# Opening by chunk: the first image loaded chunk by chunk, tiles 0 to 3 with stationary values, row sums in column groups and a listed order

## Chip, cores, metric

One core of one Trainium2 chip. The metric is device time in microseconds (us) of one execution, median of several. Ratios are the mean time of one kernel's runs over the mean of the other's runs of the same rounds, so they are not quite the ratio of the medians quoted beside them. Under 1 means faster than the kernel before.

## The reference

An attention over pooled keys is followed by a gated feed-forward block. Keys and values are the same matrix.

```
B, C, Hh, Ww = 4, 128, 384, 32;  r = 4;  d_ff = 1536
kv_pool = kv.reshape(B, H//r, r, W//r, r, C).mean(axis=(2, 4))     # 4x4 pixels -> one key
k = v = kv_pool.reshape(B, -1, C) @ w_sr                          # 768 keys an image
a = exp(q @ k^T / sqrt(C)) / row sum;   x = a @ v                 # 12288 queries an image
out = (max(x @ w_gate, 0) * (x @ w_val)) @ w_out
```

One image row of kv has 32 pixels of 512 bytes, 16 KB. A **chunk** is 128 keys, so 64 full image rows or the same number of pixels, 1 MB; an image has six. A **tile** is 512 queries, 256 KB; there are 96, numbered 0 to 95. To **turn** is to transpose, an **issue** is the instruction that starts a transfer, and a **packet** is a piece of a transfer as the trace records it.

## The kernel before

The change touches only the opening: the loads of the first image, the attention of tiles 0 to 3, and their order. Behind it runs a loop over tiles that both kernels share. Before, two chunks came together in four transfers (one for each of the four lines `dh` of the 4x4 blocks):

```python
def kv_load(b, pair, queues=(nc.sync,)):
    parts = work.tile([128, r, 2, r, C], FP32, tag="kv_in", bufs=3)
    rows = kv[b, pair * 2 * HC : (pair + 1) * 2 * HC].rearrange(
        "(hp dh) (wp h dw) c -> dh hp wp (h dw c)", dh=r, h=2, dw=r      # 32 x 4 runs of 4 KB
    )
    for dh in range(r):
        queues[dh % len(queues)].dma_start(parts[:, dh].rearrange("p h dw c -> p (h dw c)"), rows[dh])

def q_load_plain(i0, i1):                   # tiles 0-1 and 2-3: 128 runs of 4 KB, one after the other
    nc.sync.dma_start(q32, q[0, i0 * T : i1 * T, :].rearrange("(p i s) c -> p i s c", i=i1 - i0, s=NS))

def q_load_tile(i):                         # tiles 4 and 5 only
    nc.sync.dma_start(q32, q[0, i * T : (i + 1) * T, :].rearrange("(t j s) c -> j t (s c)", j=4, s=NS))
...
kv_load(0, 0, (nc.sync, nc.scalar))
nc.sync.dma_start(w_sr_f32, w_sr)
for i in range(0, GRP, 2):
    q_load_plain(i, i + 2)
for pair in range(1, NJC // 2):
    kv_load(0, pair)
for i in range(GRP, GRP + 2):
    q_load_tile(i)
```

The value step had the exponentials stationary, four matmuls of 128 x 129 for each chunk of keys, with the row sum as column 129; the tile was then normalised and turned:

```python
def values(k, jc, half):
    ...
    for i in range(2):
        s = 2 * half + i
        nc.tensor.matmul(x_ps[:, i, :], aTs[k][:, jc, s * 128 : (s + 1) * 128],
                         kv16[:, k // NST, jc, C : 2 * C + 1], ...)
...
fill(4)                                     # four idle matmuls
s1 = add_pixels(add_lines(0))               # VectorE adds the lines of two chunks at once
...                                         # turn, project, cast and turn queries, then
scores_of(0, 0)
scores_of(1, 0)
...
```

The softmax here doesn't subtract the row's maximum and nothing guards it: scores larger than these inputs give would overflow.

## Time and profile before

| | before |
|---|---|
| time | 1031.94 us (1031.92 to 1032.3) |
| TensorE busy in the profiled execution | 1022.0 of 1030.3 us |
| first score matmul starts (timeline) | 13.68 us |
| first output projection of tile 0 starts (timeline) | 37.86 us |

The last row marks the start of the shared loop. The chain of waits puts the same two starts at 13.73 and 38.02, because a step of the chain begins where the one before it ends; for comparisons below I use the timeline's figures throughout. The busy table, the stretches and the chain of this kernel are shown in the prediction. These are the two transfers of tiles 4 and 5, and the casts that wait for them (columns: durations min/median/max in ns, first and last start in us):

```profile
L109 SPq DMA_DIRECT2D q_tile<-in_q_dram x2: 583/624/664, 13.2 to 14.5; - x2
L119 POOL CAST q<-q_tile x2: 613/613/613, 24.8 to 29.4; 128x512 f16<-128x512 f32 x2
```

They were issued at 13.2 and 14.5, behind the keys, whose bytes were through at about 21 us. The casts could start only at 24.8 and 29.4, that is 4.6 us apart for 256 KB, or 57 GB/s. Nothing waited for them in this kernel, so nothing was lost. The change loads tiles 0 to 3 in the same way.

### The profile page before, as it was taken

The numbers are of one execution on the slowest core, as the hardware profiler recorded it, in microseconds if no ns is written. First come the engines' busy times: TensorE is split into PE (matmuls) and PEld (weight loads), VectorE is DVE, ScalarE is ACT, GpSimd is POOL, SyncE is SP. The second block draws the span as 40 slices with busy tenths as digits, with TensorE's granted clock in tenths as the row PEclk, the third lists the DMA queues.
The fourth block names the chain that finished last, engine by engine and source line by source line (L and its number), as shares of the span: only waits on it lengthen the run. The fifth ranks groups of instructions, "written<-read, shape, count | busy, mean of one in ns | idle before, by whom it ended". The sixth has DMA issues, their size and how long they took to land.

```text
span 1030.3 us, 20013 instructions
## 1 busy us (share of the span) xinstructions
PE 1022.0 (99%) x6560; PEld 543.7 (53%) x6560; DVE 913.0 (89%) x1676; ACT 909.3 (88%) x1745; POOL 280.5 (27%) x289
## 2 busy tenths in 40 slices
PE   7999999999999999999999999999999999999998
PEld 4555555555555555555555555555555555555555
DVE  4889898998989898998989898999888898989898
ACT  4989988888998888888888899888889988889887
POOL 1312146521211124642212121664121221111110
PEclk9999999999999999999999999999999999999999
DMA  8936396462543547726355266783653534513222
GB/s 317 120 60 81 91 191 143 77 93 42 85 65 52 78 121 161 169 52 91 52 67 85 35 85 139 144 171 57 86 65 55 73 53 67 87 33 64 34 42 53
DMA packets 328896, 93.60 MB, mean 91 GB/s; under 512 B 308568, under 2 KB 321752, under 8 KB 328792
## 3 DMA queue, kind: packets, MB, share of 16 engines
q1 hardware_dynamic: 313672, 78.24, 39.6%
q0 software_dynamic: 14688, 12.98, 11.0%
q8 instruction: 51, 0.84, 0.3%
q10 hardware_dynamic: 432, 1.11, 0.3%
q14 instruction: 53, 0.43, 0.1%
HBM read 53.94 MB, written 26.35 MB: 78 GB/s over the span
## 4 chain that ended last, share of the span: by engine, by line
PE 98%; DMA 1%; DVE 0%; ACT 0%; issue 0%; SPq 0%; ACTq 0%
PE bank_ps L298 24%; PE bank_ps L309 24%; PE bank_ps L333 23%; PE bank_ps L260 13%; PE bank_ps L249 12%; PE bank_ps L319 1%; DMA parts<-in_kv_dram 1%; PE bank_ps L182 0%; PE bank_ps L208 0%; PE bank_ps L200 0%; DVE kv_s L499 0%; DVE kv_s L460 0%; SPq L156 0%; PE bank_ps L136 0%; PE bank_ps L291 0%
## 5 line engine op out<-in xcount | busy, mean ns | idle before, releaser
L312 DVE SCALAR_TENSOR_TENSOR hT<-bank_ps,val 128x512 f16<-128x512 f32 x1152 | 758.0, 687 | 90.8 <-ACT val L302 70.3
L302 ACT CAST val<-bank_ps 128x512 f16<-128x512 f32 x1152 | 677.5, 589 | 102.2 <-PE bank_ps L298 100.2
L298 PE MATMUL bank_ps<-xT,wv 128*128 128x512 f16 x1152 | 436.6, 379 | 0.1
L309 PE MATMUL bank_ps<-xT,wg 128*128 128x512 f16 x1152 | 436.6, 379 | 0.0
L333 PE MATMUL bank_ps<-hT,wo 128*128 128x512 f16 x1116 | 423.0, 379 | 0.0
L250 ACT ACTIVATE aT<-bank_ps 128x512 f16<-128x512 f32 x576 | 345.4, 603 | 1.5 <-PE bank_ps L249 1.2
L343 POOL TENSOR_SCALAR o_sb<-o_t 128x512 f32<-128x512 f32 x93 | 138.3, 1487 | 694.0 <-DVE rinv L268 688.8
L260 PEld LDWEIGHTS <-aT 128*128 128x128 f16 x2304 | 177.0, 98 | 132.4
L260 PE MATMUL bank_ps<-kv,aT 128*128 128x129 f16 x2304 | 222.8, 220 | 0.0
L249 PE MATMUL bank_ps<-qT,kv 128*128 128x512 f16 x576 | 216.7, 379 | 0.2 <-DVE qT L139 0.2
L298 PEld LDWEIGHTS <-wv 128*128 128x128 f16 x1152 | 112.7, 98 | 132.2
L309 PEld LDWEIGHTS <-wg 128*128 128x128 f16 x1152 | 112.7, 98 | 67.3 <-DVE x L276 0.2
L333 PEld LDWEIGHTS <-wo 128*128 128x128 f16 x1116 | 109.2, 98 | 65.7
L249 PEld LDWEIGHTS <-kv 128*128 128x128 f16 x576 | 56.1, 98 | 67.8 <-issue 0.7
L276 DVE TENSOR_TENSOR x<-bank_ps,rinv 128x256 f16<-128x256 f32 x190 | 80.6, 425 | 6.6
L341 DVE STREAM_TRANSPOSE o_t<-bank_ps 128x512 f32<-128x512 f32 x93 | 65.7, 706 | 0.0
L86 POOL DMA_DIRECT2D q<-in_q_dram x84 | 46.0, 553 | 0.3 <-issue 0.3
L167 POOL TENSOR_TENSOR s<-parts 128x512 f32<-128x512 f32 x36 | 44.8, 1265 | 0.1
L268 DVE RECIPROCAL rinv<-bank_ps 128x2 f32<-128x2 f32 x192 | 28.2, 147 | 1.2 <-PE bank_ps L260 1.2
L169 POOL TENSOR_TENSOR s<-s 128x512 f32<-128x512 f32 x18 | 22.8, 1266 | 1.4
L171 POOL TENSOR_TENSOR c<-s 128x256 f32<-128x256 f32 x18 | 13.1, 725 | 1.4
L319 PEld LDWEIGHTS <-hT 128*128 128x128 f16 x144 | 10.2, 98 | 5.8
(54 smaller groups left out, 97.1 us busy)
## 6 DMA issues: line engine op xcount, KB each, us to landing
parts<-in_kv_dram SPq DMA_DIRECT2D x46, 512.0 KB, 6.5
out_dram<-o_sb SPq DMA_DIRECT2D x353, 64.0 KB, 2.2
q<-in_q_dram POOLq DMA_DIRECT2D x84, 128.0 KB, 4.8
xT<-x SPq DMA_TRANSPOSE x94, 2.5
out_dram<-o_sb SPq DMA_DIRECT2D x80, 16.0 KB, 1.5
placed<-blocks SPq DMA_DIRECT2D x9, 128.0 KB, 1.9
kvT<-placed SPq DMA_DIRECT2D x36, 32.0 KB, 1.9
parts<-in_kv_dram ACTq DMA_DIRECT2D x2, 512.0 KB, 7.4
```

Of the source, the lines that this page charges most:

```text
L86: nc.gpsimd.dma_start(q16[32 * j : 32 * (j + 1)].rearrange("t (i s) c -> t i s c", i=GRP), rows[j])
L249: nc.tensor.matmul(s_ps, kv16[:, k // NST, jc, 0:C], qT_of(k), start=True, stop=True)
L250: nc.scalar.activation(aTs[k][:, jc, :], s_ps, AF.Exp, scale=qk_scale)
L260: nc.tensor.matmul(x_ps[:, i, :], aTs[k][:, jc, s * 128 : (s + 1) * 128], kv16[:, k // NST, jc, C : 2 * C + 1], start=(jc == 0 and i == 0) ...
L276: nc.vector.tensor_tensor(x16s[k][:, 2 * half : 2 * half + 2, :], x_ps[:, :, 0:C], rinv.to_broadcast([128, 2, C]), op=ALU.mult,)
L298: nc.tensor.matmul(va_ps, wv16[:, fb * 128 : (fb + 1) * 128], xTs[k], start=True, stop=True)
L302: nc.scalar.copy(val, va_ps)
L309: nc.tensor.matmul(g_ps, wg16[:, fb * 128 : (fb + 1) * 128], xTs[k], start=True, stop=True)
L312: nc.vector.scalar_tensor_tensor(hTs[k][:, fb, :], g_ps, 0.0, vals.pop((k, fb)), op0=ALU.max, op1=ALU.mult)
L333: nc.tensor.matmul(o_banks[k], wo16[:, fb, :], hTs[k][:, fb, :], start=fb == 0, stop=fb == NFB - 1)
L341: nc.vector.transpose(o_t, o_banks.pop(k))
L343: nc.gpsimd.tensor_scalar(o_sb.rearrange("t j s c -> t s j c"), o_t.rearrange("t (s j c) -> t s j c", s=NS, j=4), 1.0 / X_SCALE**2, None, ...
```

## The change

Its intent is to start earlier and to idle less: chunks come one by one, so that the first score needs 1 MB of keys, not 2; tiles 0 to 3 use values as the stationary operand (512-column matmuls, output already turned); their row sums are made by 32-row matmuls of ones in four column groups; normalisation moves to the end as a scale by the inverse square of the sum; and all steps of the opening stand in one listed order. Cut to its core:

```diff
+    OPENING = """
+        a0 T0.3 cast1 qt1 b0 p0 a1 cast3 qt3 T0.p kvT0 qT1 pj0 qT3 key0 cast0 gate20 W0 W1 cast4
+        ...                                     # S = score, V = value, v/g = projections, U = row sums
+        g0.7 v0.5 g0.0 V1.4 v0.9 g0.2 V1.5 v0.8 g0.5 V2.4 v0.1 g0.9 S4.3 xT1 V2.5 g0.8 v0.6
+        g0.11 S4.1 g0.1 v0.10 V2.3 g0.4 S4.0 xT2 g0.6 g0.10
+    """.split()
...
+    def kv_load_lines(chunk, lines, queues=(nc.sync,)):
+        rows = kv[0, chunk * HC : (chunk + 1) * HC].rearrange(
+            "(hp dh) (wp dw) c -> dh hp wp (dw c)", dh=r, dw=r         # 16 x 8 runs of 2 KB
+        )
+        for dh in lines: ...dma_start(kv_in[0, pair][:, dh, h]..., rows[dh])
...
+    def lead_values(k, jc):
+        nc.tensor.matmul(x_banks[k], kv16[:, 0, jc, C : 2 * C], aTs[k][:, jc, :], ...)
+    def lead_sums(chunks):
+        for jc in chunks:
+            for k in range(LEAD):
+                nc.tensor.matmul(x_banks["sums"][32 * k : 32 * (k + 1), :], ones, aTs[k][:, jc, :],
+                                 ..., tile_position=(0, 32 * k))
...
-    kv_load(0, 0, (nc.sync, nc.scalar))
+    kv_load_lines(0, range(r), (nc.sync, nc.scalar))
     nc.sync.dma_start(w_sr_f32, w_sr)
-    for i in range(0, GRP, 2):
-        q_load_plain(i, i + 2)
-    for pair in range(1, NJC // 2):
-        kv_load(0, pair)
-    for i in range(GRP, GRP + 2):
-        q_load_tile(i)
+    q_load_tile(1)                              # all queries by q_load_tile now
+    q_load_tile(3)
+    kv_load_lines(1, range(3))
+    q_load_tile(0)
+    kv_load_lines(1, range(3, 4))
+    q_load_tile(2)
+    kv_load_lines(2, range(r))                  # and 3, 4, 5
+    ...
+    q_load_tile(5)
+    q_load_tile(4)
```

## The prediction

> **What bounds the kernel now.** I read the busy table first, then the chain of work that ended last, then that chain in order of time for the first 60 us, then busy time by stretch, and last the groups of instructions, for durations. The busy table and the chain:
>
> ```profile
> span 1030.3 us, 20013 instructions
> PE 1022.0 (99%) x6560; PEld 543.7 (53%) x6560; DVE 913.0 (89%) x1676; ACT 909.3 (88%) x1745; POOL 280.5 (27%) x289
> ...
> PE 98%; DMA 1%; DVE 0%; ACT 0%; issue 0%; SPq 0%; ACTq 0%
> ```
>
> TensorE is the bound over the whole program and the chain hardly leaves it. So time can come off in two ways only: fewer TensorE cycles, or less time in which TensorE issues nothing. The stretches say where the second is to be found (columns: length, then busy time of PE, PEld, DVE, ACT, POOL, granted clock, DMA share, GB/s):
>
> ```profile
> 2.00:9.00 7.00, 4.78 (x8) 1.58 (x6) 1.92 (x2) 1.49 (x2) 0.01 (x1) 1.00 0.96 352
> 9.00:13.70 4.70, 4.01 (x33) 3.28 (x34) 1.34 (x4) 1.05 (x3) 0.00 (x0) 1.00 1.03 412
> 13.70:20.50 6.80, 5.92 (x43) 3.57 (x41) 5.97 (x12) 4.83 (x11) 0.00 (x0) 1.00 1.03 409
> 20.50:26.00 5.50, 5.47 (x45) 3.96 (x45) 2.64 (x7) 4.62 (x11) 2.62 (x6) 1.00 0.72 181
> 26.00:30.00 4.00, 3.94 (x50) 3.03 (x49) 2.15 (x9) 3.15 (x7) 0.99 (x3) 1.00 1.14 129
> 30.00:38.00 8.00, 8.00 (x71) 5.01 (x70) 7.38 (x19) 7.97 (x19) 3.14 (x6) 1.00 1.33 139
> 200.00:300.00 100.00, 100.00 (x636) 52.81 (x634) 89.68 (x165) 89.44 (x172) 19.10 (x20) 1.00 0.41 62
> ```
>
> From 30 us on TensorE has no gap, and the steady loop is full. Everything that the change can win lies before 30 us. The clock is 1.00 throughout, so the clock is no part of it. The chain in order of time (start, length, what) gives the landmarks of that opening:
>
> ```profile
> 1.49 7.68 DMA parts<-in_kv_dram
> 9.17 0.04 issue
> 9.21 2.40 PE bank_ps L182 x20
> ...
> 13.73 1.11 PE bank_ps L249 x4
> ...
> 15.97 1.22 DVE kv_s L460
> 17.20 0.02 issue
> 17.22 1.29 DVE kv_s L499 x2
> ...
> 28.69 0.36 PE bank_ps L291 x4
> ...
> 38.02 0.22 PE bank_ps L333
> ```
>
> The reader should see four things. TensorE's first useful work starts at 9.21, when the first 2 MB of keys (two chunks, 128 keys each per 64 image rows) have landed. The first scores start at 13.73. The chain is on VectorE's additions from 15.97 to 18.9. The first output projection of tile 0, which is the first instruction of the regular loop that both kernels share, starts at 38.02. I measure the change by what becomes of that 38.02, since the loop behind it is full and unchanged.
>
> **What the Trainium skill says.** "TensorE: Matmul & The Clock Gate", section "Back-to-back issue gap", gives N/2.4 + 2.5 ns, 216 ns for 512 columns. The chain agrees: full matmuls follow each other at 0.21 to 0.22 us. The same section's other figure, about 131 ns in a sustained stream, is not seen here. The same page, section "Measured speedup vs the span model", reports that three matmuls of 32 output rows in different column groups run 2.38 times as fast as one after the other. "TensorEngine Tiling (Array Packing)", section "Key Properties", says that the groups are independent and that a change of tiling mode drains the engine. No run here shows either yet: the kernel before has no tiled matmul. "DMA: Bandwidth & Descriptors", section "Specifications", puts the fabric ceiling at 435 GB/s; the loads here run at 409 to 412 GB/s.
>
> **The change, part by part.**
>
> *Loads by chunk.* Before, two chunks came together in four transfers of 512 KB; now one chunk comes in four of 256 KB. VectorE's first addition started at 6.64 us (1.05 MB landed) and the third and fourth lines came at 9.17, i.e. 2.44 us per MB. Half the bytes means that lines 0 and 1 are there at about 5.4 and the whole first chunk at 6.6. Following the new order at the same rate: queries of tiles 1 and 3 at 7.4 and 8.1, chunk 1 complete at 11.3, chunk 2 at 14.5, chunk 3 at 17.0, chunk 4 at 19.6, chunk 5 at 22.2. The last one is as early as before, because the bytes are the same. I assume that 2 KB runs move as fast as the 4 KB runs did and that some 29 issues of about 0.57 us (16 us in all) don't hold up 22 us of wire.
>
> *The path to the first score.* TensorE can turn line 3 at about 6.8, when its warm-up ends. The adds b0 and p0 run on GpSimd, where a 128x512 add takes 1.27 us and a 128x256 one 0.73: 6.65 + 1.27 + 0.73 = 8.65. Turning the sum (after the queries of tile 3) to 9.4, its copy on VectorE 0.29, projection about 0.4, key copy on ScalarE 0.28: first score at about 10.5, against 13.73. Tiles 0 and 2 and chunk 1 follow; by about 13.2 TensorE has done 3.6 us of work since 6.8, and from then on it should be fed.
>
> *TensorE's work.* Terms by the chain: a full 512-column matmul 0.2155 us, a 128-column one 0.057, an f32 turn 0.1175 (16 in 1.88), a projection about 0.29. Before, from 9.2 to 38.02: 48 f32 turns 5.6, projections 1.7, 16 query turns 0.9, 24 scores 5.2, 96 value matmuls 5.5, 6 value turns 0.3, 8 output turns of tiles 0 and 1 0.4, 24 gate and value projections 5.2: 24.8 of 28.8 us, so 4.0 us without issue. After: 36 f32 turns 4.2 (VectorE now does three lines of each chunk), the 24 value matmuls of 512 columns 5.2 in place of the 96, the output turns gone, and 24 row-sum matmuls of 32 rows added. In four column groups at once those cost six steps of 0.2155 = 1.3 us; with the skill's less than perfect overlap and four drains my estimate is 2.0. The sum is 1.7 + 0.9 + 5.2 + 0.3 + 5.2 + 4.2 + 5.2 + 2.0 = 24.7. So TensorE's work does **not** fall. The gain is time without issue. In addition three scores of tile 4 (0.65 us) are done in the opening and taken from the loop.
>
> *Three walks to the start of the loop.* (1) TensorE: 24.7 + 0.65 - 3.6 = 21.7 us from 13.2: 34.9. (2) ScalarE: from about 13.6 on 25 exponentials, 12 value copies and two kept tiles, 39 at the 0.47 to 0.5 us that it takes back to back (six exponentials in 3.04), and six small ones of about 0.22: about 20.4, so 34.0. (3) The last chunk: 22.2, third-line add and pixel add 0.69 + 0.37 from line 2 on, turn, copy, projection and key copy: its key at about 24.5. Behind it the list still has 41 full matmuls (4 + 1 scores, 9 values, 24 projections, 3 scores of tile 4), 8.8 us, and the row sums, 2.0: 35.4. All three are within 1.4 us of each other, so the engines will now and then wait for one another. I choose 35.6 rather than the largest of them.
>
> *Off the path.* Normalisation leaves the opening; tiles 0 to 3 are scaled in the end by the inverse square, by a GpSimd multiply in place of one that took 1.49 us every 10.4 us; GpSimd is 27% busy. Output writes of the first group become 4 instead of 16 per tile. Neither is on a path.
>
> *Sum.* 38.02 - 35.6 = 2.4, plus 0.65 for the scores moved: 3.05 us, so 1031.94 - 3.05 = **1028.9 us**.
>
> **Rivals.** (a) The row sums run one after another: 24 x 0.2155 = 5.2 us instead of 2.0. Loop start 38.8, time 1032.1. For it: no trace here shows overlap, and each matmul reloads its weights. Against: the skill's measurement. (b) The weights come late. In the kernel before the first half of the value weights was issued at 21.0 and took about 6 us to land, the gate half 7.2; the new list asks for the first half at about 27 and the second half at about 29, where before the second half was issued only at 25.3. It is issued together with the first now, at about 20.4 to 22.9, and competes with the last keys. A stall of 1 us here gives about 1030. (c) ScalarE becomes the bound: it had 7.97 of 8.00 us busy in 30 to 38 already and gets casts, copies and early scores; with its waits for TensorE's banks (four are held by the accumulators) a loop start of 36.5 and 1029.8. (d) The list fits better than my allowance: loop start 34.3, 1027.6.
>
> **Range and chances.** (d) sets the low end, a little extended: 1027.3. (b) and (c) together lie inside the range, (a) just outside: 1031.0 at the high end. 2% are 20.6 us; the opening before 38 us can't give that, since its TensorE work alone is 24.7, and losing as much would need a wait that I see no candidate for. So faster 0.005, within 2% 0.985, slower 0.01.
>
> **What would show each step right or wrong.** First score matmul at about 10.5; first output projection at about 35.6 and no TensorE gap behind it; row sums 24 in about 2 us; last key copy at about 24.5; loads at some 410 GB/s to 22 us; gate weights not named as the releaser of a wait. The prediction fails if the row sums take over 4 us, if TensorE waits for weights, or if the loop behind, with its ScalarE backlog, shows gaps that the kernel before doesn't have.

## The result

| | before | after |
|---|---|---|
| time, median (range), 6 runs each | 1031.93 (1031.85 to 1032.88) | 1051.03 (1049.7 to 1052.52) |
| ratio, 95% interval | | 1.0184, 1.0171 to 1.0197 |
| first score starts | 13.68 | 17.92 |
| first output projection starts | 37.86 | 54.76 |

The change costs 19.1 us. By the 2% rule that still counts as the same, the class that I gave 0.985, but the time lies far outside my range of 1027.3 to 1031.0. The busy table and the chain's shares after:

```profile
span 1047.6 us, 19844 instructions
PE 1026.0 (98%) x6492; PEld 541.0 (52%) x6492; DVE 911.0 (87%) x1666; ACT 912.1 (87%) x1748; POOL 285.8 (27%) x310
...
PE 95%; DMA 5%; SPq 0%; POOL 0%; issue 0%; ACT 0%; ACTq 0%
```

TensorE is still the bound of the whole, but the chain now spends 5% with DMA (data transfers) instead of 1%. The stretches (same columns as in the prediction) say where:

```profile
2.00:9.00 7.00, 5.60 (x12) 2.23 (x10) 0.69 (x1) 1.49 (x2) 1.53 (x3) 1.00 0.99 246
9.00:13.70 4.70, 0.54 (x4) 0.27 (x4) 0.00 (x0) 0.62 (x1) 0.51 (x1) 0.87 0.55 147
13.70:20.50 6.80, 2.98 (x11) 1.43 (x11) 1.74 (x4) 2.64 (x6) 1.26 (x1) 0.50 0.83 222
20.50:26.00 5.50, 2.92 (x16) 2.54 (x17) 0.77 (x2) 0.85 (x2) 0.61 (x1) 0.50 0.54 165
26.00:30.00 4.00, 4.00 (x17) 2.05 (x16) 2.02 (x5) 2.94 (x6) 0.00 (x0) 0.56 0.98 276
30.00:38.00 8.00, 7.89 (x47) 4.38 (x46) 6.21 (x13) 6.26 (x14) 2.49 (x5) 1.00 0.78 213
200.00:300.00 100.00, 100.00 (x633) 52.72 (x631) 90.27 (x168) 89.41 (x172) 28.97 (x28) 1.00 0.47 70
```

Against the lines of before the reader sees three things. In the first three stretches the last column, 352 to 412 GB/s before, is 147 to 246. TensorE's busy time (second figure) falls to 0.54 of 4.70 us and 2.98 of 6.80. And PEclk, third from the end, falls to 0.50: from 12.4 to 29.5 us TensorE ran at half its clock, which it never did before. From 200 to 300 us TensorE is as full as before. The chain in order of time names the waits one by one (start, length, what; steps of issue under 0.1 us are left out, and what comes before the first line):

```profile
3.68 10.96 DMA q<-in_q_dram
14.65 11.24 DMA kv_in<-in_kv_dram
25.91 7.11 DMA kv_in<-in_kv_dram
33.03 12.75 DMA q_late<-in_q_dram
45.83 0.62 POOL q L98
46.48 5.43 DMA qT<-q
51.95 0.39 PE bank_ps L300
...
54.93 0.22 PE bank_ps L413
```

The opening is a string of transfers up to 46 us. The last of them is the load of a tile that the loop was to use, tile 4, whose three scores the list asks for (S4.3, S4.1, S4.0). Behind its landing come its cast (POOL), its DMA transpose (5.43 us) and only then the score that releases the rest; TensorE stood 2.8 us for it.

What I had doubted most, on the other hand, came out as predicted: the 24 row-sum matmuls are busy 1.7 us together (20 of them follow each other in 1.26 us; one after the other at 0.2155 they would take 4.3), so the column groups do overlap. And the loop keeps its pace: comparing the start of each tile's twelfth gating instruction on VectorE with that of the kernel before, the difference is 16.35 us at tile 1 and 16.35 us at tile 95, the last. I call this the **offset** below. So of the 17.3 us by which this execution's span is longer (1047.6 against 1030.3), 16.35 are lost before the loop; the other 0.9 come behind the last matmul.

One row of the profile page narrows the cause. Over 8 to 24 us of the kernel after, in 40 slices of 0.4 us (tenths of the 16 DMA engines' time, then GB/s):

```profile
DMA  9999822679422222398678999999997322229799
GB/s 236 215 225 210 169 56 77 164 215 323 118 67 97 102 102 97 123 230 323 190 169 266 343 292 246 220 230 256 271 256 164 97 102 102 102 113 225 271 348 282
```

There are stretches at 2 tenths and about 100 GB/s, a quarter of 410: something occupies four engines of sixteen while the rest has nothing to do. And even where the row says 9, the rate is 210 to 348, never 410. These look like two different faults.

One view tells why the rest has nothing to do, the waits of the issuing queue itself (its line and what it waited for; us in total, times, longest):

```profile
SPq L206 <- DMA q<-in_q_dram: 7.2, 4, 3.6
```

Issues of later keys waited 7.2 us for earlier queries to land, up to 3.6 us at a time; in the kernel before it was 0.6 us. So a slow transfer not only occupies its engines, it also holds back the issue of those behind it.

### The profile page after: what moved, and what is told of

The parts are those of the page before. It is cut to its first block, busy times and chain, and to the rows that moved or that the text cites. A ratio compares the mean times of both kernels' runs of the same rounds, so it can differ in the third digit from the quotient of the medians. Undisturbed runs are those within 1.5% of the kernel's fastest.

```text
span 1047.6 us, 19844 instructions
## 1 busy us (share of the span) xinstructions
PE 1026.0 (98%) x6492; PEld 541.0 (52%) x6492; DVE 911.0 (87%) x1666; ACT 912.1 (87%) x1748; POOL 285.8 (27%) x310
## 4 chain that ended last, share of the span: by engine, by line
PE 95%; DMA 5%; SPq 0%; POOL 0%; issue 0%; ACT 0%; ACTq 0%
PE bank_ps L391 24%; PE bank_ps L380 24%; PE bank_ps L413 23%; PE bank_ps L311 12%; PE bank_ps L300 11%; DMA kv_in<-in_kv_dram 2%; DMA q_late<-in_q_dram 1%; DMA q<-in_q_dram 1%; PE bank_ps L399 1%; DMA qT<-q 1%; PE bank_ps L265 0%; SPq L206 0%; SPq L132 0%; POOL q L98 0%; SPq L503 0%
## 5 line engine op out<-in xcount | busy, mean ns | idle before, releaser
L429 POOL TENSOR_SCALAR o_sb<-o_t 128x512 f32<-128x512 f32 x89 | 132.4, 1487 | 664.8 <-DVE rinv L319 661.0
L311 PEld LDWEIGHTS <-aT 128*128 128x128 f16 x2208 | 170.6, 98 | 130.3
L311 PE MATMUL bank_ps<-kv,aT 128*128 128x129 f16 x2208 | 215.3, 220 | 0.0
L327 DVE TENSOR_TENSOR x<-bank_ps,rinv 128x256 f16<-128x256 f32 x184 | 78.1, 425 | 6.6
L427 POOL TENSOR_TENSOR o_sb<-o_t,lead_scale 128x512 f32<-128x512 f32 x4 | 4.2, 1046 | 33.2 <-DVE rinv L319 25.7
```

Of the source, the lines that this page charges most:

```text
L327: nc.vector.tensor_tensor(x16s[k][:, 2 * half : 2 * half + 2, :], x_ps[:, :, 0:C], rinv.to_broadcast([128, 2, C]), op=ALU.mult,)
L429: nc.gpsimd.tensor_scalar(to, o_by, 1.0 / X_SCALE**2, None, op0=ALU.mult)
```

## The theories

**Queries on four engines.** The change reads tiles 0 to 3 with an access pattern whose outermost count is 4 (`j t (s c)`). The Trainium skill, "DMA: Bandwidth & Descriptors", section "Why a DMA increments its semaphore by 16 and not by 1", says that the number of engines is the largest k of at most 16 that divides the slowest dimension of both access patterns. Here that is 4. I had not looked at this section. By that rule and the measured 410 GB/s my estimate is 2.6 us for 256 KB on four engines instead of 0.64, and what is queued behind waits.

**Keys slow in their new layout.** 16 x 8 runs of 2 KB, rather than 32 x 4 runs of 4 KB.

**Rivals.** (R1) The new order and the 29 issues hold the wire (the sixteen DMA engines together) up. (R2) The half clock is the cause, not a consequence, so idle matmuls would mend it. (R3) The new list and the row sums cost the time and the loads only move with it.

## The experiments

All give the reference's result. e11_side and e14_pitch have two timed runs each, the others four or five. "Offset" is that of the profiled execution, at the last tile where no tile is named. Packet times are medians of the trace's packets of 2 KB and more, and rates those of all packets, in stretches of 3 us. A packet's record names neither its transfer nor its engine, so that queries and keys are told apart by packet size or by time.

| run | kernel it edits | time us | ratio, 95% | first score | output proj. |
|---|---|---|---|---|---|
| e1_q_plain | after | 1044.76 | 1.0128, 1.0112 to 1.0144 | 11.98 | 48.55 |
| e2_kv_pairs | after | 1046.78 | 1.0140, 1.0124 to 1.0157 | 18.90 | 52.20 |
| e3_both | after | 1035.47 | 1.0031, 1.0016 to 1.0046 | 13.93 | 40.37 |
| e1b_q_split | after | 1041.41 | 1.0091, 1.0076 to 1.0106 | 15.22 | 48.19 |
| e4_before_q4 | before | 1045.37 | 1.0129, 1.0114 to 1.0145 | 16.59 | 50.89 |
| e4b_before_q16 | before | 1038.80 | 1.0065, 1.0051 to 1.0079 | 13.81 | 44.29 |
| e5_before_2k | before | 1033.43 | 1.0021, 1.0006 to 1.0036 | 14.42 | 38.79 |
| e6_both_late | after | 1034.76 | 1.0028, 1.0013 to 1.0043 | 13.06 | 39.17 |
| e7_warm | after | 1033.15 | 1.0011, 0.9994 to 1.0028 | 13.19 | 38.10 |
| e8a_halves | after | 1036.68 | 1.0041, 1.0027 to 1.0055 | 10.59 | 41.62 |
| e8_mended | after | 1033.88 | 1.0013, 1.0000 to 1.0026 | 10.69 | 38.16 |
| e9_mended_warm | after | 1033.89 | 1.0018, 1.0004 to 1.0032 | 11.02 | 38.30 |
| e10_no_s4 | after | 1032.68 | 1.0006, 0.9993 to 1.0018 | 11.00 | 36.08 |
| e13_q4_first | after | 1033.48 | 1.0016, 1.0002 to 1.0029 | 11.02 | 37.82 |
| e11_side | after | 1033.73 | 1.0017, 0.9998 to 1.0035 | 10.35 | 39.15 |
| e14_pitch | after | 1039.61 | 1.0068, 1.0038 to 1.0097 | 11.80 | 44.79 |

### Mending one fault at a time: e1_q_plain, e2_kv_pairs, e3_both

e1_q_plain reads tiles 0 to 3 as 128 runs, one after the other (the output rows are permuted to match):

```diff
-        nc.sync.dma_start(q32, q[...].rearrange("(t j s) c -> j t (s c)", j=4, s=NS))
+        if i < GRP:
+            nc.sync.dma_start(q32, q[...].rearrange("(p s) c -> p (s c)", s=NS))
```

> The changed kernel with the queries of tiles 0 to 3 read as 128 runs of 2 KB, partition by partition, in place of four groups of 32 rows; the output rows are placed accordingly. Bytes, run length (2 KB) and order of issue stay. Theory A (the four-group read goes to 4 of the 16 DMA engines and each later transfer waits behind it on these four): the queries land within about 1 us of each other's wire time, first score at about 11 to 12 us instead of 17.9, TensorE never falls to half clock, time down by at least 8 us from 1051, to about 1036 to 1042 (tiles 4 and 5 are still read by four groups). Theory B (2 KB runs and twice as many transfers are slow whatever engine they are on): the loads stay at about 220 GB/s, first score stays after 15 us, time stays within 3 us of 1051.

Measured: 1.0128, offset +10.4 us. The first score moves from 17.92 to 11.98, as expected; the time of 1036 to 1042 and the full clock are not reached (1044.76, and 0.55 from 13.7 to 20.5 us). From 7 to 8 us, when the first queries come, a packet takes 88 ns, but from 9 to 27 us, mostly keys, it is 116 to 136 ns, and all 16 engines are busy at 260 to 292 GB/s from 6 to 27 us. So the four-engine fault is real and the second fault stands by itself.

e2_kv_pairs leaves the queries as they are and loads keys by pairs as before:

```diff
-    kv_load_lines(0, range(r), (nc.sync, nc.scalar))
+    kv_load(0, 0, (nc.sync, nc.scalar))
     ... # queries 1, 3, 0, 2, then
-    kv_load_lines(2, range(r)) ...
+    kv_load(0, 1)
+    kv_load(0, 2)
```

> The changed kernel with keys read two chunks at a time in 4 KB runs as in the kernel before, and the queries of tiles 0 to 3 still by four groups. Theory A: the queries still block four engines; chunks 2 to 5 still land late, the time stays above 1045. Theory B: the loads run at about 400 GB/s again and the time falls to about 1032 to 1036.

Measured: 1.0140, offset +13.8. The key packets of 4 KB take 159 ns ahead of the queries, 250 to 273 ns while query packets are under way (to 23.3 us), and 159 ns again from 24 us on: the queries on four engines also slow the keys beside them. Issues of keys waited 8.8 us for queries.

e3_both makes both edits (tiles 4 and 5 still on four engines).

> The changed kernel with both: queries of tiles 0 to 3 in 128 runs, keys two chunks at a time in 4 KB runs. What is left of the change is the order of the arithmetic. Both theories: loads at about 400 GB/s until 22 us. If the arithmetic is as I worked it out, the time is 1028 to 1033; the late read of tiles 4 and 5 by four groups (landing at about 29 in the kernel before) may hold the start of the loop at about 37.5, i.e. 1031. If the new order itself is bad, above 1036.

Measured: 1.0031, above the 1028 to 1033 us expected. The loads run at 399 to 411 GB/s from 9 to 21 us, 4 KB packets 162 to 167 ns, and no issue of keys waits for queries. The stretch from 13.7 to 20.5 us in the three kernels, in this order:

```profile
13.70:20.50 6.80, 6.02 (x28) 4.17 (x29) 2.95 (x7) 3.33 (x8) 0.58 (x1) 0.55 1.07 277
13.70:20.50 6.80, 3.43 (x15) 2.27 (x16) 1.65 (x4) 2.33 (x6) 0.46 (x1) 0.50 1.04 253
13.70:20.50 6.80, 6.57 (x37) 4.70 (x38) 3.40 (x9) 5.01 (x13) 2.07 (x4) 0.74 1.03 410
```

The two edits remove 6.3 and 4.3 us of the time alone, but 15.6 together (1051.03 to 1035.47): either fault alone is enough to keep the opening waiting. The new list, the row sums and all other parts of the change are in this kernel too, so R3 can hold at most the remaining 3.3 us. R1 fails as far as the order goes: with the queries still in single transfers of 256 KB and the keys in pairs the wire is full. This run has 12 issues fewer; the number of issues is tested in e8_mended.

### The fault alone, in the kernel before: e4_before_q4, e4b_before_q16, e5_before_2k

e4_before_q4 puts only the four-group read into the kernel before:

```diff
-        nc.sync.dma_start(q32, q[0, i0 * T : i1 * T, :].rearrange("(p i s) c -> p i s c", ...))
+        for i in range(i0, i1):
+            nc.sync.dma_start(q32[:, i - i0]..., q[...].rearrange("(t j s) c -> j t (s c)", j=4, s=NS))
```

> The kernel BEFORE with one thing of the change: the queries of tiles 0 to 3 read by four groups of 32 rows, one transfer a tile, in place of two transfers in 4 KB runs (output rows placed accordingly). Theory A (four-group reads sit on 4 engines and hold up every later transfer): loads fall below 300 GB/s behind the queries, the regular loop starts 10 us or more later, time 1040 or more. If it is only the 2 KB key reads or the new order, the time stays within 2 us of 1032.

Measured: 1.0129, offset +13.03 at tile 1 and after. So the four-group read alone, moved into the kernel before (with the output rows placed to match), loses 13.4 us (1031.97 to 1045.37). Its stretches show the same signs as the kernel after:

```profile
13.70:20.50 6.80, 1.82 (x8) 0.53 (x8) 0.74 (x2) 2.68 (x5) 0.00 (x0) 0.77 1.05 247
20.50:26.00 5.50, 1.76 (x12) 1.12 (x12) 1.36 (x5) 0.00 (x0) 0.00 (x0) 0.50 1.04 285
```

TensorE is busy 1.8 of 6.8 us and then 1.8 of 5.5, and the clock falls to 0.77 and 0.50. Issues of keys waited 9.0 us for queries, and the 4 KB key packets took 266 to 278 ns while query packets were under way (to 23.5 us).

e4b_before_q16 reads the very same rows into the same places with the same 2 KB runs, but each tile by four transfers of 32 rows, whose outermost count is 32:

```diff
+            rows = q[...].rearrange("(t j s) c -> j t (s c)", j=4, s=NS)
+            for j in range(4):
+                nc.sync.dma_start(q32[32 * j : 32 * (j + 1), i - i0]..., rows[j])
```

> The kernel BEFORE with the same query rows to the same places in the same 2 KB runs as the version of it that cost 13.4 us, but each tile's read issued as four transfers of 32 rows (outermost count 32) in place of one transfer of four groups of 32 (outermost count 4). If the outermost count sets how many engines a transfer is spread over (theory A): the loads stay near 400 GB/s and the time is 1031.5 to 1034. If the row order or the 2 KB runs of the queries are at fault, it stays near 1045.

Measured: 1.0065, offset +6.43. The stretches:

```profile
9.00:13.70 4.70, 3.89 (x32) 3.23 (x33) 1.29 (x4) 1.05 (x3) 0.00 (x0) 1.00 0.47 143
20.50:26.00 5.50, 3.55 (x16) 3.25 (x16) 2.98 (x5) 0.53 (x2) 0.00 (x0) 0.57 1.02 411
```

Query packets take 84 to 88 ns and the keys behind them come at 411 GB/s and 159 ns, not 285 and 266 to 278. So it is the outermost count, not the rows or the run length, that made the queries slow. The keys are issued only behind the last query here (from 13.9 us), so that this run doesn't show both side by side; e3_both does, with queries on all engines and keys between 9 and 12 us at 399 GB/s. The time of 1031.5 to 1034 that I expected is missed, and the other half of the loss is a new one: 16 issues for 64 KB each, of about 0.42 us, cannot fill the wire (143 GB/s at 9 to 13.7 us). They take 10.8 us, 3.6 of them waits for keys to land, and the other keys are issued behind them. Here R1, which failed above, is the right answer for 64 KB transfers.

e5_before_2k reads the keys of the first image in 2 KB runs, one chunk's half of each 4 KB at a time (two transfers for a line):

```diff
-            queues[...].dma_start(parts[:, dh]..., rows[dh])
+            ...                                     # other images as before
+            for h in range(2):
+                queues[...].dma_start(parts[:, dh, h]..., rows[dh][:, :, h * r * C : (h + 1) * r * C])
```

> The kernel BEFORE with the first image's keys read in 2 KB runs, two transfers a line in place of one in 4 KB runs; nothing else. Theory B' (2 KB key runs move at 275 GB/s, as seen in the version with plain queries, where a packet took 120 to 130 ns against 159 for twice the bytes): loads at some 280 GB/s instead of 410, last keys at about 30 us instead of 22, time up by 5 to 8 us. Rival: the slow packets come from the new kernel's chunk layout (16 runs side by side per line and engine stride of 64 KB), not from the length; then the rate stays near 400 and the time within 2 us of 1032.

Measured: 1.0021, offset +0.93; packets of 2 KB take 84 to 87 ns, 389 GB/s from 12 to 21 us. So 2 KB instead of 4 KB costs 5% of the rate (389 against 410) and does not explain 275 GB/s. "Short runs" falls as the cause of the second fault.

### Another way to mend the queries: e1b_q_split

```diff
+        for j in range(4):
+            (nc.scalar if i < GRP and j % 2 else nc.sync).dma_start(q32[32 * j : 32 * (j + 1)], rows[j])
```

> The changed kernel with each four-group query read (tiles 0 to 5) issued as four transfers of 32 rows, half of those of tiles 0 to 3 on ScalarE's queue: same rows to the same places, same 2 KB runs, keys unchanged. Theory A: a read whose outermost count is 32 goes to all 16 engines; time down to about 1030 to 1038, and better than the version with only tiles 0 to 3 mended, since tiles 4 and 5 come some 6 us sooner. Theory B: within 3 us of 1051.

Measured: 1.0091, offset +9.8 at tile 1, which misses the 1030 to 1038 us expected. It tells little: ScalarE's own table load stood 10.4 us behind the issues put on its queue, so two things changed at once, and the keys are still slow. I used e1_q_plain's way from here on.

### Mended as far as the loads go: e6_both_late, e7_warm

e6_both_late is e3_both with tiles 4 and 5 in four 32-row transfers each:

```diff
+        else:
+            for j in range(4):
+                nc.sync.dma_start(q32[32 * j : 32 * (j + 1)], rows[j])
```

> The version with 128-run queries and paired 4 KB keys, with tiles 4 and 5 also on all engines (four transfers of 32 rows each). If the queries of tile 4 set the start of the loop at 40.5 (they landed at 31.5, and the first score of tile 4 came at 37.55), they now land at about 25, the wait of TensorE for them is gone, and the time falls by 0.3 to 1.5 us from 1035.5. If TensorE's own work was the limit there (it issued with few gaps from 17 to 40 us), it stays within 0.5.

Measured: 1.0028. Tile 4's cast starts at 27.4 instead of 31.5, and the offset is +0.82 at tile 1 (+1.95 in e3_both), but the time is only 0.7 us better (0.3 by the ratios), which the runs don't tell from none.

e7_warm adds idle matmuls to e6_both_late, so that TensorE does not stand idle while it waits for keys:

```diff
-    fill(4)
+    fill(6)
-    a0 T0.3 cast1 qt1 b0
+    a0 T0.3 F F cast1 qt1 b0        # F: an idle matmul of 384 columns
```

> The previous version with four idle matmuls more ahead of the first keys and behind their first turn, so that TensorE is not idle from 7 to 10 us. If half clock (granted 0.5 from 10.4 to 17.3 us in the version with both loads mended) costs what I think: some 4.5 us of issued work done at half rate, i.e. about 2 us. Clock 1.00 throughout, time about 2 us less than without them, near 1032. If the arrival of data and not the clock is the limit until 17 us, no change.

Measured: 1.0011, offset -0.25 at tile 1 and +0.05 at tile 95. The clock is 1.00 throughout (in e6_both_late 0.91 at 9 to 13.7 us and 0.81 at 13.7 to 20.5). The clock is worth 1.6 us here (1034.76 to 1033.15; the four times of each don't overlap). So R2 is right in a small way: the half clock has a cost of its own, but it follows from idleness, and it is not the main cause, since e3_both removed 15.6 us while its clock still fell from 10.4 to 17.3 us.

### Chunk by chunk, but at full rate: e8a_halves, e8_mended, e9_mended_warm

e8a_halves is e1_q_plain with a chunk cut as before, as one half of each 4 KB of 128 image rows:

```diff
-        rows = kv[0, chunk * HC : ...].rearrange("(hp dh) (wp dw) c -> dh hp wp (dw c)", ...)
+        rows = kv[0, pair * 2 * HC : ...].rearrange("(hp dh) (wp h dw) c -> dh h hp wp (dw c)", ..., h=2)
```

> The changed kernel with 128-run queries and keys still chunk by chunk in 2 KB runs, but with the chunks cut as in the kernel before (each chunk takes every second 2 KB run of a line over 128 image rows, instead of all eight of a line over 64 rows). If the slow key packets (120 to 130 ns, 275 GB/s) come from the side-by-side pattern (theory C): packets 84 ns, loads at 390 GB/s, last keys at about 23 instead of 31 us, and the time falls from 1044.8 to about 1033 to 1036 (tiles 4 and 5 still on four engines, which held the loop to 40.5 us in the version with paired keys). If 2 KB key runs are slow in this program anyway: no change from 1044.8.

Measured: 1.0041. The rate is 365 to 397 GB/s from 9 to 21 us with 84 to 87 ns a packet, and the first score starts at 10.59. The time is 8.1 us less than that of e1_q_plain, from which it differs in the layout of the key reads alone. Tile 4's queries still come on four engines (their cast at 31.2), and TensorE waits 2.4 us for them.

e8_mended adds the 32-row transfers for tiles 4 and 5 to e8a_halves.

> The same with tiles 4 and 5 on all engines too: every load of the change as I took it to be when I predicted, chunk by chunk at about 390 GB/s. If the rest of the prediction was right (first score at 10.5, loop start at 35.6), 1028 to 1030.5. If the clock falls to half behind TensorE's early gaps, 1 to 2 us more, 1030 to 1032.

Measured: 1.0013, offset -0.26 and, from tile 7 on, +0.13. This is the kernel that loads as I had predicted for the change: first score at 10.69 (predicted 10.5), the clock 1.00 throughout, TensorE idle for 0.2 us in all from 13.7 to 30 us. But the loop starts no earlier than before, and 1033.88 us lie above both expectations. The timeline of TensorE shows one long gap, with its releaser in brackets, and the chain shows what led to it (issues left out):

```profile
35.34 0.39 PE L303 MATMUL bank_ps<-qT,kv 128*128 128x512 f16 x1 [1.75 <-DMA qT<-q]
```

```profile
23.86 5.06 DMA q_late<-in_q_dram
29.08 0.62 POOL q L98
29.71 5.58 DMA qT<-q
35.34 0.39 PE bank_ps L303
```

It is the score S4.3 again, which waits 1.75 us for tile 4. Part of this is the mending's own doing: the eight small transfers of tiles 5 and 4 were issued from 18.3 to 24.2 us, tile 4's last one at 23.86.

The record shows one more thing of this kernel. Its median time is 1.8 us above that of before in the same rounds, but the median span of its program only about 0.6 (1030.9 against 1030.3). Time less span is 1.9 to 3.1 us in its five runs, and 1.7 to 1.9 in every run of before. What fills this remainder no trace here shows; it lies outside the span.

e9_mended_warm adds small idle matmuls (128 to 384 columns) to e8_mended.

> The same with five small idle matmuls (one or two of 384 columns, three of 128) in TensorE's early gaps, to hold the clock. If the clock fell to half without them: 1 to 1.5 us faster than without, about 1028.5 to 1030. If it did not fall: up to 0.7 us slower.

Measured: 1.0018. There is no gain, as there was no half clock left to avoid.

### The rest of the gap: e10_no_s4, e13_q4_first

e10_no_s4 strikes the three scores of tile 4 from the list of e8_mended; the loop, which does every score that is not done, does them.

```diff
-        ... g0.9 S4.3 xT1 V2.5 g0.8 v0.6 g0.11 S4.1 g0.1 v0.10 V2.3 g0.4 S4.0 xT2 g0.6 g0.10
+        ... g0.9 xT1 V2.5 g0.8 v0.6 g0.11 g0.1 v0.10 V2.3 g0.4 xT2 g0.6 g0.10
```

> e8_mended with the three scores of tile 4 taken out of the opening list; the loop, which does every score not yet done, does them itself. Theory (the wait of 1.75 us for tile 4's turned queries at 33.6 to 35.3 is what e8_mended lacks of the prediction): the wait vanishes, three matmuls of 0.65 us leave the opening, the first output projection of tile 0 comes at 38.16 - 1.75 - 0.65 = 35.8, and since the 0.65 come back in the loop the time falls by 1.75 against e8_mended: about 1032, ratio to before 0.9985 or less, at best 0.998. Rival (ScalarE or VectorE, not the queries, sets the loop start): the loop start moves by less than 0.7 and the ratio stays at 1.001; then another wait shows at 33 to 37 us. Second rival: tile 4's queries are simply awaited at the loop's first scores and the same wait appears some us later.

Measured: the gap is gone and the first output projection starts at 36.08, 2.08 us earlier than in e8_mended and 1.78 earlier than before:

```profile
26.00:30.00 4.00, 4.00 (x34) 1.40 (x32) 1.34 (x3) 3.44 (x8) 0.85 (x2) 1.00 0.73 140
30.00:38.00 8.00, 7.93 (x38) 3.32 (x38) 7.93 (x15) 7.93 (x16) 6.96 (x24) 1.00 0.94 117
```

TensorE is busy 7.93 of 8.00 us (6.25 in e8_mended). The theory's mechanism holds, and neither rival does. The time does not follow: 1032.68, ratio 1.0006 with an interval that includes 1. In the profiled execution, the slowest of the five, the offset is -1.57 at tile 2, -1.20 at tile 8 and -1.02 at tile 95, so 0.55 us go in the loop. Behind the end of its last matmul this execution takes 5.53 us to the end, against 3.15 in before and 3.81 in e8_mended; the last packets of the output come up to 3.4 us after that matmul (1.7 in before), beside a 16 KB transfer of the instruction queue that took 1.55 us. Whether that transfer is the cause is not shown. The five timed runs spread over 1031.69 to 1033.47, so a gain of half a microsecond could not be shown in any case.

e13_q4_first keeps the three scores and loads tile 4 ahead of chunk 5:

```diff
+    q_load_tile(4)
     kv_load_lines(5, range(r))
     q_load_tile(5)
-    q_load_tile(4)
```

> e8_mended with tile 4's queries issued ahead of chunk 5 of the keys instead of behind it and tile 5; the three scores of tile 4 stay in the list. Theory (as for e10): the cast of tile 4 starts about 2.5 us earlier (26.5 instead of 29.08), its turned queries are there at about 32.8, before TensorE asks for them at 33.6, no wait; chunk 5 and with it the last key come 0.7 us later. Loop start about 36.6, ratio about 0.9990. Rival (last key sets the loop start): the loop start moves later by 0.7 from 38.16 less the wait, and no better than 37.5. Rival (another engine): unchanged 38.2.

Measured: 1.0016, first output projection at 37.82, not 36.6. The wait for tile 4 is gone here too, but in this execution the clock fell (0.72 at 9 to 13.7 us, 0.94 at 13.7 to 20.5; 1.00 in e8_mended), after a wait of 1.56 us for a query cast on ScalarE. So this run says no more than that the wait can be avoided in this way; what it is worth is not measured.

### Why the chunk layout is slow: e11_side, e14_pitch

Two layouts of one line of a chunk were known, both with 128 runs of 2 KB: slow in the change (16 image rows, 64 KB apart, 8 runs side by side in each) and fast in e8_mended (32 rows, also 64 KB apart, 4 runs in each, every second 2 KB). e11_side takes the left or right half of 32 rows, so that four runs lie side by side:

```diff
-            "(hp dh) (wp h dw) c -> dh h hp wp (dw c)", dh=r, h=2, dw=r
+            "(hp dh) (h wp dw) c -> dh h hp wp (dw c)", dh=r, h=2, dw=r
```

> e8_mended with one thing changed in the keys' transfers: a chunk is the left or right half of 128 image rows[...] (keys are only permuted, the result is the same). If side by side is what makes the chunk layout of the change slow: packets of 2 KB take 120 to 130 ns, some 275 GB/s, the first score is about 1 us later and the loop start at least 4 us later than in e8_mended. If the 64 KB between the engines' rows (with 16 image rows a line instead of 32) is the cause: 84 ns and 390 GB/s as in e8_mended, and the same time.

Measured: 84 ns a packet, 345 to 384 GB/s from 9 to 21 us, ratio 1.0017. Runs side by side are not the cause. That left the 16 whole rows, or a distance: if the engines share out the rows in order, which no trace here shows, an engine has one of 16 rows or two of 32, and neighbours start 64 or 128 KB apart. e14_pitch takes every second group of rows out of 128, so 16 whole rows 128 KB apart:

```diff
-            "(hp dh) (wp h dw) c -> dh h hp wp (dw c)", dh=r, h=2, dw=r
+            "(hp h dh) (wp dw) c -> dh h hp wp (dw c)", dh=r, h=2, dw=r
```

> e8_mended with one thing changed in the keys' transfers: a chunk takes every second group of four image rows out of 128 rows (the even or the odd groups), whole rows.[...] If the distance of 64 KB is what slows the change's keys: packets of 2 KB at 84 to 90 ns, some 390 GB/s, and the time of e8_mended. If the whole row by one engine does it: 120 to 130 ns, some 275 GB/s, last key 5 us or more later and the time 1 us or more above e8_mended.

Measured: 124 to 132 ns a packet and 265 to 277 GB/s from 9 to 27 us, ratio 1.0068, offset +6.37. The stretch from 15 to 21 us in e8_mended, e11_side and e14_pitch, in this order:

```profile
15.00:21.00 6.00, 6.00 (x39) 3.69 (x38) 4.70 (x11) 5.02 (x12) 0.00 (x0) 1.00 1.05 388
```

```profile
15.00:21.00 6.00, 6.00 (x30) 3.20 (x29) 4.05 (x9) 4.35 (x10) 0.00 (x0) 0.79 1.02 361
```

```profile
15.00:21.00 6.00, 6.00 (x30) 3.88 (x29) 2.99 (x7) 3.79 (x8) 0.00 (x0) 0.60 1.06 266
```

The DMA share (second from the end) is full in all three; only the rate differs. So it is neither the run length (e5_before_2k), nor the neighbourhood of four runs (e11_side), nor the distance of 64 KB, which my expectation for this run offered as one of two causes. What slow layouts have in common is a source pattern of 16 rows with eight runs in each; fast are 32 rows with four runs, and the queries of e1_q_plain with 128 runs in one sequence. By what mechanism 16 x 8 is slower **stays open**. The pattern may also change which engine writes which partitions, and since no packet's record names its engine or its address, that rival on the writing side is untested too; two runs that I did not make would be 16 rows with four runs each, and 16 x 8 with a gap between the runs.

## Why the prediction was wrong

- **The step that failed** is in the part "Loads by chunk": "I assume that 2 KB runs move as fast as the 4 KB runs did and that some 29 issues … don't hold up 22 us of wire". I applied the rate of the old access patterns to new ones. The queries of tiles 0 to 3 moved on four engines (e4_before_q4 against e4b_before_q16), and held back the issues behind them by 7.2 us; the keys moved at some 275 GB/s in place of 410 (e1_q_plain, e14_pitch; 8.1 us between e1_q_plain and e8a_halves). The assumption as I worded it was nearly right: 2 KB runs reached 389 GB/s (e5_before_2k), and in e8_mended all the issues of the change, and six more, kept the wire at 385 to 391 GB/s from 9 to 21 us. I had asked about the run length and the number of issues, and not about the shape of the pattern.
- **The rivals** left it out too. I considered late weights, but no late query or key, and wrote of a large loss that it "would need a wait that I see no candidate for". The kernel's own trace had the candidate: the two q_tile transfers at 57 GB/s.
- **The half clock** was not in the prediction: "the clock is no part of it". It is no part while TensorE is fed. From 12.4 to 29.5 us of the kernel after, each matmul took double its time because TensorE had been idle.
- **The path to the first score** was right in its working: 10.5 predicted, 10.69 in e8_mended where the loads run at 385 to 391 GB/s from 9 to 21 us.
- **Row sums and TensorE's work**: 2.0 us estimated, 1.7 measured. Rival (a) is refuted. That TensorE's work "does not fall" holds too (1021.5 us busy in e8_mended, 1022.0 before). The four drains allowed for in the 2.0 us were not measured apart.
- **The three walks** came out late. The last key was predicted at about 24.5; in e8_mended its copy starts at 25.65, of which the run length's 5% explain about 1 us of 20. The walks also lacked a fourth: tile 4's load, cast and transpose, which ends at 35.3 in e8_mended and later in every other kernel whose TensorE waits for it; in e6_both_late, e7_warm and e13_q4_first, where it is earlier, TensorE doesn't wait. Without it (e10_no_s4) the loop starts 1.78 us earlier than before. I had predicted 2.4 with the three scores of tile 4 done by then; with their 0.65 us added e10_no_s4 would start at 36.7, where I had 35.6.
- **Sum**: the 0.65 us for the three scores of tile 4 are not won when they are waited for. And what an earlier loop start is worth in the end was taken as one to one; in e10_no_s4, 0.55 of 1.57 us went in the loop, and the end took 2.4 us longer than before.
- **The loop** has no new gaps in the change as it ran (offset 16.35 at tile 1 and tile 95), and weights are no releaser of note: right. In some mended kernels the loop loses a little (the offset grows from 1.95 to 3.12 in e3_both and from -0.12 to 1.00 in e9_mended_warm); I didn't follow up why.

What the change could have won is thus small, about 1.5 us of 1032 at most by the offset of e10_no_s4, and no version that I ran is faster than the kernel before beyond doubt.

## What to carry to other kernels

When a change alters the access pattern of a load, take the rate from a transfer with that same pattern, not from the wire's mean: look for one in the trace of before, and compare its time from issue to landing with its bytes. Ask first of each pattern what its outermost count is. And when a load is late, look for its second cost, which is here the clock, and for the consumer furthest back in a fixed order, here the scores of tile 4: an item placed early in a list turns a late transfer from hidden to exposed.

## What the Trainium skill lacked or had wrong

- "DMA: Bandwidth & Descriptors", section "Why a DMA increments its semaphore by 16 and not by 1": the rule for the number of engines is right (stretches at 2 tenths and about 100 GB/s for the four-group queries; 84 ns packets and a loss of 6.4 instead of 13.0 us with 32-row transfers). It does not say what such a transfer does to others beside and behind it: 4 KB packets of the keys took 250 to 278 ns instead of 159, with all engines busy, while its packets were under way, and issues of keys waited 8.8 and 9.0 us for it to land (e2_kv_pairs, e4_before_q4).
- The same page's measured case of copies that are slow by their row pitch begins at 512 KiB. It has none like this one, with all engines busy and rows 64 or 128 KB apart: 16 rows of eight 2 KB runs each took 116 to 136 ns a packet (260 to 283 GB/s, e1_q_plain and e14_pitch from 9 to 27 us), 32 rows of four runs 84 to 87 ns (345 to 391 GB/s from 9 to 21 us).
- "TensorE: Matmul & The Clock Gate", section "Back-to-back issue gap": of its two figures for 512 columns the runs show 216 ns, and nowhere the 131 ns of a sustained stream (in the full loop of the kernel before, 200 to 900 us, no 512-column matmul is followed by the next in less than 215 ns). "TensorEngine Tiling (Array Packing)" is confirmed on the overlap of column groups: 20 matmuls of 32 rows in 1.26 us, against 4.3 one after the other.
